# A windowed-attention and maxout kernel whose score products are cut into quarters of 32 queries, with the mixing products cut to the same weight shape

## Chip, cores and metric

The kernel runs on one core of one Trainium2 chip. The metric is the device time of one execution in microseconds (us). TensorE is called PE, and its weight loads PEld; VectorE is DVE, ScalarE is ACT, GpSimd is POOL and SyncE is SP. Differences of less than about 1% can hardly be told from no change here.

## The reference

Attention with a causal window of 128 keys and a linear bias, then a maxout layer, all in float32. There are 8 batches, 8 heads, 576 positions, 64 features a head.

```python
B, H, S, D = q.shape                                   # 8, 8, 576, 64
scores = scale * np.matmul(q, k.transpose(0, 1, 3, 2))
rel = pos[:, None] - pos[None, :]
mask = (rel >= 0) & (rel < 128)
scores = np.where(mask, scores + bias[None], -1000000000.0)
attn = softmax(scores)
attn_out = np.matmul(attn, v)
x = attn_out.transpose(0, 2, 1, 3).reshape(B * S, H * D)
h = np.maximum(np.maximum(x @ w1, x @ w2), x @ w3)     # 512 -> 768
return h @ w_out                                       # 768 -> 512
```

A query thus needs its own key and the 127 keys before it.

## The kernel before

**Attention.** A task is one batch and one pair of heads; there are 32. In a task the 576 queries are taken in blocks of 128 (i = 0 to 3) and a last one of 64. The last blocks of two tasks are joined into one step (i = NB = 4), so that two tasks make 9 steps, a batch 18 and the kernel 144. `steps` (L307) lists them, and they are worked off in pairs (s, s + 1).

`products` (L314) makes the scores of a pair of steps. For each step and each head j of the pair of heads it makes one product for each half h of the queries: 64 queries (the weights, `lhsT`, 64 features by 64 queries) with a range of keys (the moving operand), into PSUM partitions d to d + 63. The features of head j lie in partitions j * 64 to j * 64 + 63, so a step's four products take the four quarters of the PE array: two row halves (j) by two column halves (h). In a step with i = 0 each product takes 128 keys; in the other steps it takes the 192 keys from 128 before its first query to its last query; in batch 0 every second pair of steps is `whole`, has its own banks and takes 256 keys for i from 1 to 3. The columns of PSUM are the keys of the block before, then the block's own.

`score` (L339) merges the two key blocks: a masked copy on DVE (L347, L350) puts the score with a key of the block before over the place of each key after the query. Then a DVE instruction adds the bias and takes the row minimum (L361). `exps` is the exponential on ACT (L373), `sums_of` and `normalise` (L387, L392) divide by the row sum, `turn` (L400) transposes two steps' weights with four 128 by 128 PE products, ACT copies them (L404), and POOL splits them with two masked selects (L420, L424) into the part for the block's own keys and the part for the block before.

**Mixing** is the product of the weights with v. Batch 0 uses `mix` (L445), with 128 by 64 weights; this function is not touched. Batches 1 to 7 use `mix_rows` (L456): its inner `add` (L465) takes half of the keys (r, partitions r * 64 and on: the row half) of one block i and one head j (the column half: `lhsT` is 64 keys by 64 features of v), and moves 64 to 256 columns of queries through it into the PSUM bank of r. ACT and DVE then add the two banks (L500, L501). `MIX` says after which step of a task which blocks are mixed. A task takes 26 calls of `add` on average.

**Maxout and output.** `unit` (L613) makes one of 7 products of a fast matrix scheme, of 6 (for the output: 9) PE products of 128 by 128 weights with 288 columns (L641), in a float32 form rounded to a high and a low part. Their operands come from `split` on ACT and DVE (L514, L515) and subtractions (L518); results leave through ACT copies (L601, L650) and DVE (L599, L604, L605, L607). The weight tiles are streamed from DRAM by POOL's queue (L267).

**The order.** `events` is a list in which each piece has a due time in units of a step: for the pair of steps s, the products at s + 0.002, the transposes LAG_T = 4 steps later, the mixing LAG_X = 6 steps after the step it belongs to; the units of the batch before are spread evenly between. So PE's stream in batches 1 to 7 is: some 40 to 60 products of units, then a stage of mixing, scores and transposes, then units again. Up to step 46 (early in the third batch) the framework's planner orders PE's instructions by its own costs and by priority; from there on `pe` (L282) keeps PE to the program's order. Loads of q, k and v are issued on SP's queue (L295, L300).

Of the kernel before, what the change touches and what calls it, by code (L numbers as in the profile page):

```python
# [16 lines left out]
PSUM = bass.MemoryType.PSUM  # L17

NEG = 1.0e30
LOAD_I = 1  # L20
LAG_T, LAG_X = 4, 6
SHIFT = (0, 2, 4)
# [10 lines left out]
def attention_maxout_kernel(  # L33
# [11 lines left out]
    nc = tc.nc  # L45
    P = 128
    B, NP, _, _, S = qk.shape
    C, D = S // 2, P // 2
# [4 lines left out]
    NB = S // P  # L53
# [59 lines left out]
    def slopes(hp):  # L113
        for h in (2 * hp, 2 * hp + 1):
            nc.scalar.activation(bias[:, h, :], dist[:, 0], AF.Copy, scale=slope(h))
        nc.gpsimd.affine_select(  # L116
            out=bias0[:, 2 * hp:2 * hp + 2], in_=bias[:, 2 * hp:2 * hp + 2], pattern=[[0, 2], [-1, P]],
            compare_op=ALU.is_ge, fill=-NEG, base=0, channel_multiplier=1,
        )
# [162 lines left out]
    def pe(ins):  # L282
        if fixed:
            tc.keep_in_program_order(ins)
# [3 lines left out]
    qkt, vt = {}, {}  # L288
# [25 lines left out]
    def products(s):  # L314
        whole = s < n_steps and s % 4 == 2
        ps = [ps_m.tile([P, 512], F32, name=f"ps_m{j}") for j in range(2)] if whole else [scores[:, j] for j in range(2)]
        for a, (t, i) in enumerate(steps[s:s + 2]):
            banks[s + a] = [x[:, a * 2 * P:(a + 1) * 2 * P] for x in ps], None if whole else a
            for j in range(2):
                for h in range(2):  # L320
                    d = h * D
                    u, q0 = (t, i * P + d) if i < NB else (t + h, S - D)
                    if i == NB:
                        k0, k1 = q0 - P, S
                    elif i == 0:
                        k0, k1 = 0, P
                    elif whole:
                        k0, k1 = (i - 1) * P, (i + 1) * P
                    else:
                        k0, k1 = q0 - P, q0 + D  # L330
                    o = a * 2 * P + k0 - (i - 1) * P
                    pe(nc.tensor.matmul(  # L332
                        ps[j][d:d + D, o:o + k1 - k0],
                        lhsT=qkt[u][j * D:(j + 1) * D, 0, q0:q0 + D],
                        rhs=qkt[u][j * D:(j + 1) * D, 1, k0:k1],
                        start=True, stop=True, skip_group_check=True,
                    ))
# [118 lines left out]
    def mix_rows(t, blocks):  # L456
        b, hp = tasks[t]
        first = blocks[0] == 0
        if first:
            xp[t] = ps_x.tile([P, 2, 512], F32, name="ps_x")  # L460
            room[t] = 4 - len(blocks)
        x, vv, last = xp[t], vt[t], slice(t % 2 * D, (t % 2 + 1) * D)
        slot = lambda q: (q + room[t]) % 4 * P

        def add(r, j, i, rhs, o, start):  # L465
            k = slice(r * D, (r + 1) * D)
            pe(nc.tensor.matmul(  # L467
                x[j * D:(j + 1) * D, r, o:o + rhs.shape[1]], lhsT=vv[k, i, j * D:(j + 1) * D], rhs=rhs[k],
                start=start, stop=True, skip_group_check=True,
            ))  # L470

        for i in blocks:
            w = pp[t, i]
            low = (0, D if i else 0)
            if i == NB:
                for j in range(2):
                    add(1, j, i, w[:, j, 0, last], slot(i), False)
                continue
            whole = i < NB - 1 and slot(i) + P == slot(i + 1)
            for r in range(2):  # L480
                for j in range(2):
                    if whole:
                        y = w[:, j].rearrange("p a b -> p (a b)")
                        add(r, j, i, y[:, low[r]:(P + D, 2 * P)[r]], slot(i) + low[r], i == 0)
                    else:
                        add(r, j, i, w[:, j, 0, low[r]:], slot(i) + low[r], i == 0)
            if whole:
                continue
            for r in range(2):
                for j in range(2):  # L490
                    if i < NB - 1:
                        add(r, j, i, w[:, j, 1, :(D, P)[r]], slot(i + 1), False)
                    else:
                        add(r, j, i, pp[t, NB][:, j, 1, last], slot(NB), True)
        if first and hp % 2 == 0:
            xk[b, hp // 2] = xk_p.tile([P, 2, S], F32, name=f"xk{hp // 2}")
        c0, c1 = blocks[0] * P, min(S, (blocks[-1] + 1) * P)
        o = xk[b, hp // 2][:, hp % 2, c0:c1]
        y = x[:, :, slot(blocks[0]):slot(blocks[0]) + c1 - c0]
        nc.scalar.copy(out=o, in_=y[:, 0])  # L500
        nc.vector.tensor_tensor(out=o, in0=y[:, 1], in1=o, op=ALU.add)  # L501
# [157 lines left out]
    def at(when, what, *args):  # L659
        events.append((when, len(events), what, args))  # L660
# [3 lines left out]
    for s, (t, i) in enumerate(steps):  # L664
        c = s + shift[tasks[t][0]]
        if i == LOAD_I and t + 2 < len(tasks):
            at(c - 0.4, load, t + 2)
        if i == NB - 1 and t + 1 < len(tasks):
            at(c - 0.4, load_v, t + 1)
        if i == 0 and 0 < t < NP:  # L670
            at(c - 1, slopes, t)
            if t % 2 == 0:
                at(c - 1, slopes_t, t // 2)
        at(c + 0.04, score, s)
        at(c + 0.3, exps, s)
        if s % 2 == 0:
            at(c + 0.002, products, s)
            at(c + LAG_T + 0.003, turn, s)
        else:
            at(c + 1.1, sums_of, s)  # L680
            at(c + 1.5, normalise, s)
# [83 lines left out]
```

## Time and profile before

| | |
|---|---|
| median of 3 runs | 785.2 us (781.43, 785.20, 785.99) |
| the profiled execution | 782.06 us, its span 780.4 us |
| granted TensorE clock | 0.997 |
| PE busy | 750.2 us, 96% of the span |
| DVE, ACT, POOL busy | 554.6, 520.9, 185.5 us |
| score products (L332) | 1152 records, 69.1 us with some of them in flight |
| mixing products (L467) | 1456 records, 55.2 us with some of them in flight |
| unit products (L641) | 4032 records of 128 by 128 weights and 288 columns |
| DMA | 185 MB, 237 GB/s |

How to read it: a group names the line, the engine, the operation, what it writes and reads, then for PE the size of the weights (rows * columns), then the moving operand (partitions x columns) and the count; behind the bar come the busy time, the mean duration of one in ns, and idle time before it with what ended that. Products overlap in PE, so a group's busy time is the time in which at least one of them is in flight, and the mean of one is a latency. A float32 product of the program appears as two records, each with its own weight load (transposes appear as one).

A row of the timeline has the start in us, the time to the last one's end, the engine, line and form, and the count of instructions merged into the row. A row of the table by stretches has the stretch, its length, and for each engine the busy time and the count of instructions that touch the stretch; the last columns are the granted clock, DMA's share and GB/s.

### The profile page before, as it was taken

Reading aid. Unit: us, or ns where it says so; the run is one execution under the profiler, and the core shown is the slowest. Engines: PE = TensorE matmul, PEld = TensorE weight load, DVE = VectorE, ACT = ScalarE, POOL = GpSimd, SP = SyncE. Lnnn points to the kernel's source line nnn. Section 1 sums busy time; section 2 is a strip of 40 time slices with the busy share of each in tenths; the row PEclk is TensorE's granted clock in tenths of the full one; section 3 lists DMA queues with packets and bytes.
Section 4 is the critical chain, followed back from the end, with each engine's and each line's share of the span. In section 5 each row is a group of like instructions: output and inputs, shape, how many; then the busy total and the mean of one; then the engine's idle time right before and its main releaser. Section 6 shows DMA issues by size and latency. Waiting matters only on the chain.

```text
span 780.4 us, 19465 instructions
## 1 busy us (share of the span) xinstructions
PE 750.2 (96%) x7286; PEld 684.6 (88%) x7291; DVE 554.6 (71%) x1722; ACT 520.9 (67%) x1684; POOL 185.5 (24%) x388
## 2 busy tenths in 40 slices
PE   7888999999999999999999999999999999999997
PEld 3556878889998998999999998999999998999987
DVE  5888899885767747794777747794777757674562
ACT  6898787776767756776677666776677757542331
POOL 4331222211322122221222122311223122301100
PEclk9999999999999999999999999999999999999999
DMA  7862768584887569874888468974888567856851
GB/s 242 291 256 72 243 259 311 211 294 144 286 298 261 176 207 294 294 276 136 281 287 281 166 221 294 300 255 140 282 296 274 166 223 258 281 172 211 295 184 60
DMA packets 41678, 184.95 MB, mean 237 GB/s; under 512 B 4592, under 2 KB 13552, under 8 KB 32368
## 3 DMA queue, kind: packets, MB, share of 16 engines
q0 software_dynamic: 18144, 115.61, 44.4%
q1 hardware_dynamic: 23296, 67.97, 24.9%
q8 instruction: 57, 0.93, 0.5%
q14 instruction: 37, 0.30, 0.1%
q10 hardware_dynamic: 144, 0.13, 0.1%
HBM read 157.74 MB, written 25.95 MB: 235 GB/s over the span
## 4 chain that ended last, share of the span: by engine, by line
PE 64%; DVE 16%; ACT 8%; issue 7%; DMA 3%; POOL 1%; SPq 0%; POOLq 0%; DVEq 0%; ACTq 0%
PE ps_m L641 48%; PE ps_s L332 4%; PE pt L400 4%; PE ps_x L467 4%; DVE hs L515 4%; DVE hq L605 2%; ACT p L373 2%; DVE t L604 2%; DVE t L518 2%; PE pt L191 2%; DMA qk<-in_qk 1%; PE ps_m L191 1%; DMA wt<-keep 1%; DMA hs<-in_w_all 1%; DVE xk L501 1%
## 5 line engine op out<-in xcount | busy, mean ns | idle before, releaser
L641 PE MATMUL ps_m<-xs,wt 128*128 128x288 f32 x3024 | 430.3, 298 | 10.5 <-DVE hq L599 3.6
L641 PEld LDWEIGHTS ps_m<-xs,wt 128*128 128x128 f32 x3024 | 408.3, 189 | 18.2 <-DVE hq L599 5.3
L650 ACT COPY t<-ps_m 128x288 f32<-128x288 f32 x264 | 103.2, 394 | 83.0 <-PE ps_m L641 80.2
L641 PE MATMUL ps_m<-hs,ow 128*128 128x288 f32 x1008 | 140.9, 296 | 3.4 <-DVE hs L515 1.7
L641 PEld LDWEIGHTS ps_m<-hs,ow 128*128 128x128 f32 x1008 | 134.3, 188 | 6.5 <-ACT t L650 2.6
L420 POOL TENSOR_SCALAR_AFFINE_SELECT pp<-pr 128x256 f32<-128x256 f32 x112 | 54.2, 484 | 312.7 <-ACT pr L404 183.3
L373 ACT ACTIVATE p<-s,st 128x128 f32<-128x128 f32 x288 | 115.0, 403 | 17.2 <-DVE st L361 14.6
L267 POOL DMA_DIRECT2D wt<-keep x126 | 68.0, 539 | 210.9 <-PE ps_m L641 201.5
L392 ACT ACTIVATE p<-p,st 128x128 f32<-128x128 f32 x252 | 85.4, 395 | 23.8 <-DVE st L380 23.5
L604 DVE TENSOR_TENSOR t<-ps_m,t 128x288 f32<-128x288 f32 x144 | 64.8, 453 | 49.3 <-PE ps_m L641 31.3
L361 DVE CUSTOM_DVE_ANT_0 s<-ps_s,bias 128x128 f32<-128x128 f32 x240 | 60.8, 286 | 11.7 <-POOL bias L116 4.7
L605 DVE TENSOR_TENSOR hq<-t,hq 128x288 f32<-128x288 f32 x144 | 65.4, 460 | 2.6
L332 PE MATMUL ps_s<-qk 64*64 64x192 f32 (+1 forms) x1088 | 63.4, 317 | 2.6 <-DMA qk<-in_qk 2.0
L514 ACT CAST hs<-hq 128x288 fp32r<-128x288 f32 x96 | 41.0, 432 | 23.3 <-DVE hq L605 20.8
L373 ACT ACTIVATION_READ_ACCUMULATOR p<-s,st 128x1 f32 x288 | 55.8, 194 | 0.0
L467 PE MATMUL ps_x<-pp,v 64*64 64x64 f32 (+3 forms) x1456 | 55.2, 274 | 0.0
L501 DVE TENSOR_TENSOR xk<-ps_x,xk 128x256 f32<-128x256 f32 (+3 forms) x56 | 25.5, 455 | 41.8 <-ACT xk L500 41.8
L467 PEld LDWEIGHTS ps_x<-pp,v 64*64 64x64 f32 x1456 | 42.3, 133 | 10.8 <-issue 9.2
L424 POOL TENSOR_SCALAR_AFFINE_SELECT pp<-pr 128x256 f32<-128x256 f32 (+1 forms) x112 | 48.6, 434 | 1.1
L400 PE MATMUL pt<-plus,p 128*128 128x128 f32 x288 | 47.5, 286 | 1.2 <-DVE wt L181 0.5
L332 PEld LDWEIGHTS ps_s<-qk 64*64 64x64 f32 x1088 | 39.9, 134 | 9.8 <-issue 3.9
L400 PEld LDWEIGHTS pt<-plus,p 128*128 128x128 f32 x288 | 30.2, 140 | 19.4 <-issue 12.6
(89 smaller groups left out, 800.0 us busy)
## 6 DMA issues: line engine op xcount, KB each, us to landing
wt<-keep POOLq DMA_DIRECT2D x63, 1024.0 KB, 7.3
wt<-keep POOLq DMA_DIRECT2D x63, 768.0 KB, 5.8
qk<-in_qk SPq DMA_DIRECT2D x31, 576.0 KB, 5.3
hs<-in_w_all SPq DMA_DIRECT2D x12, 1023.6 KB, 6.5
v<-in_v SPq DMA_DIRECT2D x32, 320.0 KB, 5.8
keep<-wt SPq DMA_DIRECT2D x9, 1024.0 KB, 5.6
outT<-t SPq DMA_DIRECT2D x64, 144.0 KB, 1.8
keep<-wt SPq DMA_DIRECT2D x9, 768.0 KB, 4.7
```

What stands on the lines that cost most here:

```text
L267: nc.gpsimd.dma_start(wts[n, a], keep[n % 9][a])
L332: pe(nc.tensor.matmul(ps[j][d:d + D, o:o + k1 - k0], lhsT=qkt[u][j * D:(j + 1) * D, 0, q0:q0 + D], rhs=qkt[u][j * D:(j + 1) * D, 1, k0:k1] ...
L361: nc.vector.tensor_tensor_reduce(out=x, in0=ps[j][:, P:2 * P], in1=below, scale=-0.125, scalar=3.0e38, op0=ALU.add, op1=ALU.min, accum_out ...
L373: nc.scalar.activation(p[:, j], x, AF.Exp, bias=st[:, 0, a, j:j + 1], scale=-1.0, accum_out=st[:, 1, a, j:j + 1])
L392: nc.scalar.activation(p[:, j], p[:, j], AF.Copy, scale=st[:, 2, a, j:j + 1])
L400: pe(nc.tensor.transpose(out=pt[:, a, j], in_=p[:, j], identity=ident))
L420: nc.gpsimd.affine_select(out=old, in_=src, pattern=[[-x, n] for x, n in pat], compare_op=ALU.is_gt, fill=0.0, base=0, channel_multiplier=1,)
L467: pe(nc.tensor.matmul(x[j * D:(j + 1) * D, r, o:o + rhs.shape[1]], lhsT=vv[k, i, j * D:(j + 1) * D], rhs=rhs[k], start=start, stop=True, s ...
L604: nc.vector.tensor_tensor(out=s, in0=ps, in1=e, op=ALU.add)
L605: nc.vector.tensor_tensor(out=h, in0=s, in1=h, op=ALU.max)
L641: pe(nc.tensor.matmul(ps, lhsT=lt, rhs=rt, start=i == 0 and k in (0, 1, 4), stop=i == len(pairs) - 1, skip_group_check=True,))
L650: nc.scalar.copy(out=e, in_=ps)
```

## The change

In `products` each step's queries are taken in quarters of Q = 32 instead of halves of 64. The weights become 64 features by 32 queries, and the key range, where it is not 128 or 256 as above, becomes the 160 keys from 128 before the quarter's first query to its last query. A step has 8 products instead of 4. In the joined last step (i = NB) the quarters d = 0 and 32 belong to the first task and d = 64 and 96 to the second.

In `mix_rows` (batches 1 to 7) each product with 64 by 64 weights becomes two with 64 by 32 weights and the same moving columns. `mix` of batch 0 stays as it is.

```diff
+Q = 32
...
             for j in range(2):
-                for h in range(2):
-                    d = h * D
-                    u, q0 = (t, i * P + d) if i < NB else (t + h, S - D)
-                    if i == NB:
-                        k0, k1 = q0 - P, S
-                    elif i == 0:
+                for d in range(0, P, Q):
+                    u, q0 = (t, i * P + d) if i < NB else (t + d // D, S - D + d % D)
+                    if i == 0:
                         k0, k1 = 0, P
-                    elif whole:
+                    elif whole and i < NB:
                         k0, k1 = (i - 1) * P, (i + 1) * P
                     else:
-                        k0, k1 = q0 - P, q0 + D
+                        k0, k1 = q0 - P, q0 + Q
                     o = a * 2 * P + k0 - (i - 1) * P
                     pe(nc.tensor.matmul(
-                        ps[j][d:d + D, o:o + k1 - k0],
-                        lhsT=qkt[u][j * D:(j + 1) * D, 0, q0:q0 + D],
+                        ps[j][d:d + Q, o:o + k1 - k0],
+                        lhsT=qkt[u][j * D:(j + 1) * D, 0, q0:q0 + Q],
                         rhs=qkt[u][j * D:(j + 1) * D, 1, k0:k1],
                         start=True, stop=True, skip_group_check=True,
                     ))
...
         def add(r, j, i, rhs, o, start):
             k = slice(r * D, (r + 1) * D)
-            pe(nc.tensor.matmul(
-                x[j * D:(j + 1) * D, r, o:o + rhs.shape[1]], lhsT=vv[k, i, j * D:(j + 1) * D], rhs=rhs[k],
-                start=start, stop=True, skip_group_check=True,
-            ))
+            for m in range(j * D, (j + 1) * D, Q):
+                pe(nc.tensor.matmul(
+                    x[m:m + Q, r, o:o + rhs.shape[1]], lhsT=vv[k, i, m:m + Q], rhs=rhs[k],
+                    start=start, stop=True, skip_group_check=True,
+                ))
```

## The prediction

> **What bounds the kernel now.** I read the page first, then the busy time by stretch of about one batch, then who PE waits for, then the chain that ended last, and then single stages of PE in narrow windows.
>
> ```profile
> span 780.4 us, 19465 instructions
> PE 750.2 (96%) x7286; PEld 684.6 (88%) x7291; DVE 554.6 (71%) x1722; ACT 520.9 (67%) x1684; POOL 185.5 (24%) x388
> ```
>
> ```profile
> core 0: us, PE busy (x) PEld busy (x) DVE busy (x) ACT busy (x) POOL busy (x), PEclk, DMA share, GB/s
> 0.00:90.00 90.00, 77.91 (x603) 52.04 (x609) 70.17 (x216) 72.86 (x223) 30.95 (x64) 0.98 0.62 219
> 90.00:177.00 87.00, 82.37 (x820) 72.94 (x819) 77.75 (x211) 67.15 (x197) 20.65 (x36) 1.00 0.74 265
> ...
> 264.00:351.00 87.00, 86.16 (x898) 81.23 (x895) 61.82 (x205) 59.97 (x204) 21.37 (x46) 1.00 0.74 247
> ...
> 698.00:780.00 82.00, 74.76 (x552) 73.21 (x550) 38.23 (x94) 24.38 (x62) 7.43 (x14) 1.00 0.54 181
> ```
>
> From 177 to 698 us PE is busy 86 of every 87 us, and nothing else comes near it (DVE 62). In that stretch it waits for others only this much:
>
> ```profile
> PE ps_m L641 <- DVE hq L599: 3.6, 6, 0.6
> PE ps_m L641 <- ACT t L650: 0.5, 2, 0.3
> PE ps_m L641 <- DVE hs L515: 0.3, 1, 0.3
> ```
>
> So there a nanosecond of PE is nearly a nanosecond of span. In 0 to 90 PE, ACT and DVE share the limit, and in 90 to 177 DVE has 78 of 87. After 698 there are no scores and no mixing.
>
> The groups that the change touches:
>
> ```profile
> L332 PE MATMUL ps_s<-qk 64*64 64x192 f32 x840 | 55.4, 329 | 2.1 <-DMA qk<-in_qk 1.4 <-DVE st L361 0.7
> L467 PE MATMUL ps_x<-pp,v 64*64 64x192 f32 x364 | 30.3, 344 | 0.0
> L467 PE MATMUL ps_x<-pp,v 64*64 64x128 f32 x364 | 29.9, 274 | 0.0
> L467 PE MATMUL ps_x<-pp,v 64*64 64x64 f32 x644 | 24.9, 218 | 0.0
> L332 PE MATMUL ps_s<-qk 64*64 64x128 f32 x248 | 15.2, 277 | 0.5 <-DMA qk<-in_qk 0.5
> ```
>
> Their means (218 to 344 ns) are latencies that overlap; the pace has to be read from starts. Each float32 product of the program is two records: 144 steps of 4 products give the 1152 score records of L332. Here is one stage of two score steps, 16 records of 192 keys. The first column is the start. The rows come from ever later narrow windows, so each shows the start of the next group:
>
> ```profile
> 263.22 0.88 PE L332 MATMUL ps_s<-qk 64*64 64x192 f32 x16
> ...
> 263.44 0.51 PE L332 MATMUL ps_s<-qk 64*64 64x192 f32 x8
> ...
> 263.60 0.51 PE L332 MATMUL ps_s<-qk 64*64 64x192 f32 x8
> ...
> 263.76 0.34 PE L332 MATMUL ps_s<-qk 64*64 64x192 f32 x4
> ...
> 264.03 0.33 PE L400 MATMUL pt<-plus,p 128*128 128x128 f32 x1
> ```
>
> Four records start together at 263.22, 263.44, 263.60 and 263.76. The four 64 by 64 tiles of the array (two row halves by two column halves) thus run side by side, each streaming 192 columns in 0.16 us, or 0.83 ns a column. The first group takes 0.22: the extra 0.05 or 0.06 is the first weight load, which nothing hides. A stage with mixing and scores:
>
> ```profile
> 301.98 0.90 PE L467 MATMUL ps_x<-pp,v 64*64 64x192 f32 x28
> 302.69 0.74 PE L332 MATMUL ps_s<-qk 64*64 64x128 f32 x16
> 303.36 0.66 PE L400 MATMUL pt<-plus,p 128*128 128x128 f32 x4
> ```
>
> ```profile
> 302.47 0.42 PE L467 MATMUL ps_x<-pp,v 64*64 64x128 f32 x14
> 302.69 0.28 PE L332 MATMUL ps_s<-qk 64*64 64x128 f32 x2
> ...
> 302.80 0.63 PE L332 MATMUL ps_s<-qk 64*64 64x128 f32 x12
> ...
> 302.91 0.52 PE L332 MATMUL ps_s<-qk 64*64 64x192 f32 x8
> ```
>
> Groups of 128 keys follow 0.11 us apart (302.69, 302.80, 302.91), the same 0.83 to 0.86 ns a column. So the stage is bound by what each tile streams, and scores follow mixing without a gap.
>
> **The change part by part.** *Scores.* A step's four products of 64 queries with 192 keys become eight of 32 queries with 160. If the array runs eight 64 by 32 tiles side by side as it runs four now, a tile streams two records of 160 columns, 2 x 0.133 = 0.267 us, where it streams 2 x 0.16 = 0.32. That is 0.053 us less for each step with i from 1 to 4. A step with i = 0 keeps its 128 keys, and so do the 256 keys of batch 0's whole steps. A batch has 18 steps, 14 of them with i over 0: 14 x 0.053 = 0.75 us a batch, and 5.2 us for batches 1 to 7.
>
> *What of it reaches the end.* Once or twice a batch DVE sets the pace:
>
> ```profile
> 296.43 0.46 DVE t L604
> ...
> 302.03 0.38 DVE t L518
> ...
> 306.51 5.05 PE ps_m L641 x36
> ...
> 337.84 0.47 DVE t L604
> ...
> 344.91 5.09 PE ps_m L641 x36
> ```
>
> The chain runs on DVE and ACT from 296.4 to 306.5 and from 337.8 to 344.9; what PE saves in the two stages inside is waited for anyway. The first of them has one step with i over 0 (the 0.11 pace of the other is shown above), the second one or two. I take 3 of the 14 as lost, bounds 0 and 4. That leaves 11 x 0.053 x 7 = 4.1 us. Batch 1's scores lie in 90 to 177, where DVE is almost as full as PE; half of its 0.6 goes too, which leaves 3.8. For batch 0 (7 steps of 192 keys, at most 0.4 us, on a stretch shared by three engines) I take nothing.
>
> *Mixing.* Every product with 64 by 64 weights becomes two with 64 by 32 that stream the same columns. A batch's 208 records of L467 become 416 and its 144 score records become 288. On eight tiles each tile streams what it did, so the stage keeps its length. The DVE, ACT and POOL work behind it is the same.
>
> *Weight loads.* The first load is for 32 columns instead of 64: 0.05 becomes 0.03, once in each of some 65 stages, a gain of 1.7 us. Against it, four more tiles have to be started. The price of a start is bounded from both sides by this stage:
>
> ```profile
> 301.98:302.01 0.03, 0.03 (x4) 1.00 0.53 205
> ```
>
> Four start within 0.03 us, about 7 ns each, so four more cost 0.03 a stage, 1.8 us in all: the two cancel. From the other side, the densest longer stretch is the 14 records between 302.47 and 302.69, 0.22 / 14 = 16 ns, but there the tiles were full and streaming, so it is no proof of a limit. Eight tiles of 64-column products (0.053 us each) want a start every 7 ns. I take 7 to 9 ns, since the row with four starts is the one in which tiles are waiting for the sequencer; that costs the 64-column stretches 0 to 1 us over the kernel, and I take 0.
>
> *Instruction supply.* 2608 more products and as many loads are fetched (the row: packets, MB, share of the DMA engines):
>
> ```profile
> q8 instruction: 57, 0.93, 0.5%
> ```
>
> That is 16 KB a packet and 64 bytes for each of the 14577 records of PE and PEld, so 0.33 MB is added, spread over 780 us and hidden behind PE's long 128 by 128 runs. Bounds: nothing, or, if a packet came late in a stage, up to the shortest landing on the page's list, 1.8 us each time. I take nothing: the stages of now show no gap inside.
>
> *Order.* Up to about a third of the batches (step 46, some 225 us) the framework's planner, which counts each product's cost, orders PE. Twice the products can move other work around there. Bounds from the stages of that stretch: some lie alone with 0.2 us of switching in and 0.25 out; a handful more or fewer of them is 2 us either way. I take 0.
>
> **Sum:** 782.06 (the profiled execution's own time; 1.7 us of it lie around its span of 780.4) - 3.8 = 778.3. The runs shown have a median of 785.2, 3.1 above that execution, so on their scale 785.2 - 3.8 = 781.4; I say 781. That is 0.5%, less than the 1% that a measurement of this kernel can tell from no change.
>
> **The rivals.** *Everything lands* (faster by over 1%): the scores' 5.2, batch 0's 0.4, the loads' 1.7 without the stagger, and the rest that a record costs beside its columns (0.11 us in the row for 128 columns, against 128 x 0.83 = 0.106: an estimated 4 ns) falling away with the halved loads for the 64-column products of mixing, 644 / 4 = 161 on each tile, 0.6 us: 7.9 us, 777. For it speaks the full PE; against it the two DVE stretches. Chance 0.15.
>
> *Starts are the limit* (slower). One mechanism: PE cannot start products as fast as eight tiles eat them. A batch now has 352 records in about 10.9 us of streaming (scores: 14 x 0.32 + 4 x 0.213 = 5.3; mixing: 4 tasks, in each of which a tile of the second row half streams 832 columns by the ranges in mix_rows, 4 x 832 x 2 x 0.83 ns = 5.55). With 704 records at p ns each it is over that from 15.5 ns on, and over 1% slower (7.9 us in 7 batches) from 17 ns on. The stage above has 44 records from 301.98 to the start of its last group, 302.91 + 0.16 = 303.07: 25 ns. If that were a limit of starting, 704 x 25 = 17.6, + 6.7 x 7 = 47 us, 832. Against it stand the stretch at 16 ns and the burst at 7. Half way, at 20.5 ns: 14.4, + 3.5 x 7 = 25 us, 810. The Trainium skill has a rule of this kind: TensorE: Matmul & The Clock Gate, Wait — 56ns, not 53.3ns?, puts the least distance of two starts at about 25 ns however few the columns. The trace shows less for products in different tiles, so by this trace it does not hold between tiles. By it the time would be the 832 above.
>
> The chance of this rival is 0.14.
>
> *Quarters take turns* (slower). Nothing in the trace runs four column tiles in one row half. If only two can stream, a step of eight tiles takes 0.533 for 0.32 (0.427 for 0.213 at i = 0), 3.8 us more a batch, and mixing doubles, 5.55 more: 9.4 x 7 = 66 us, 851. Against it: two column halves already take different columns at the full pace. Chance 0.06.
>
> *The planner's part* goes wrong by more than 8 us in the first 225: 793 to 800. Chance 0.05. That the change does not do what it says (the shapes stay) I exclude from the diff.
>
> **How the numbers follow.** The forecast, within 1%, has the remaining 0.60. Faster by over 1% is the rival in which everything lands, 0.15. Slower by over 1%: 0.14 + 0.06 + 0.05 = 0.25. The likeliest one's own range is 777.5 to 787 (no loss to DVE, or starts at 16 ns: 704 x 16 = 11.3, + 2.5 us). The range that should hold 8 in 10 reaches down to 774 (everything, and 3 us of the planner) and up to 800 (starts at 18.5 ns, or the planner's case); the far ends of two rivals, 810 and more, are left out.
>
> **What would show it.** Right: L332 has 2304 records of 64x160, 64x128 and a few 64x256 in form 64*32, L467 has 2912; eight start within some 0.05 us; a stage like that at 263.22 is 1.03 - 0.11 = 0.92 us from the last L641 before it to the first L400; a stage's mixing part keeps its 0.71 us; a batch from 264 us on takes some 0.6 us less. Wrong: groups of four starts, or starts evenly 15 ns or more apart in the mixing; stages longer than now; an idle gap inside a stage; waits of PE on DVE growing by more than 0.2 us a batch; the first 177 us moved by more than 2 us.

## The result, and the profile after

The changed kernel takes 790.74 us (median of 5 runs, 789.76 to 792.33) where the kernel before takes 783.75 in the same comparison (5 runs, 781.43 to 785.99): a ratio of 1.0098, 95% interval 1.0072 to 1.0124. It is 7.0 us, 1%, slower; the forecast was 0.5% faster. 790.74 lies in the range of 774 to 800, but nearer to cases that I had given little chance.

Lines of the page after, and of its view of groups with the shapes kept apart:

```profile
span 788.1 us, 24680 instructions
PE 753.5 (96%) x9899; PEld 688.7 (87%) x9899; DVE 555.9 (71%) x1722; ACT 521.3 (66%) x1684; POOL 188.4 (24%) x388
...
q8 instruction: 78, 1.28, 0.7%
```

```profile
L330 PE MATMUL ps_s<-qk 64*32 64x160 f32 x1680 | 52.9, 303 | 1.8 <-DMA qk<-in_qk 1.1 <-DVE st L359 0.7
...
L466 PE MATMUL ps_x<-pp,v 64*32 64x128 f32 x728 | 32.2, 274 | 0.0
L466 PE MATMUL ps_x<-pp,v 64*32 64x192 f32 x728 | 30.5, 333 | 0.0
L466 PE MATMUL ps_x<-pp,v 64*32 64x64 f32 x1288 | 30.2, 220 | 0.0
```

The shapes are as written, and DVE, ACT and POOL have the same count of instructions and, within 3 us, the same busy time. PE is 3.3 us busier in a span that is 7.7 longer. (Numbers of lines shift by 1 or 2 against the kernel before: L332 is L330, L467 is L466, L641 is L640, L400 is L398, L650 is L649, L599 and L607 are L598 and L606.)

**Where the time went.** A batch begins for PE with a stage of scores alone; the timeline of PE has it, after:

```profile
263.79 0.29 PE L640 MATMUL ps_m<-hs,ow 128*128 128x288 f32 x1
264.01 0.78 PE L330 MATMUL ps_s<-qk 64*32 64x160 f32 x32
264.71 0.44 PE L398 MATMUL pt<-plus,p 128*128 128x128 f32 x2
...
352.38 0.37 PE L330 MATMUL ps_s<-qk 64*32 64x160 f32 x8
```

The next such row of the kernel before:

```profile
349.93 0.39 PE L332 MATMUL ps_s<-qk 64*64 64x192 f32 x4
```

Before, a batch is 349.93 - 263.22 = 86.71 us; after, 352.38 - 264.01 = 88.37. The other batches up to 617 us are alike (86.7 to 86.8 and 88.3 to 88.4). Four whole batches lose 6.4 us, the part of a batch from 184 to 264 us loses 1.0 and the tail 0.5; the first 184 us lose nothing. So the loss is not where I had looked for the planner's influence, the first third.

**What is in a batch.** First, the stages. The score stage above is 264.71 - 263.79 = 0.92 us from the last unit product, 0.11 less than before, and the eight first records fall within 0.05 us: the scores do what was forecast. Most stages with mixing do not. The one that was 301.98 to 303.36 is now

```profile
302.90 1.03 PE L466 MATMUL ps_x<-pp,v 64*32 64x192 f32 x53
303.71 0.31 PE L330 MATMUL ps_s<-qk 64*32 64x128 f32 x2
...
303.81 0.72 PE L330 MATMUL ps_s<-qk 64*32 64x128 f32 x28
304.46 0.66 PE L398 MATMUL pt<-plus,p 128*128 128x128 f32 x4
```

Its mixing takes 0.81 us (302.90 to 303.71) instead of 0.71, and the stage 1.56 instead of 1.38. Measured from the last unit product before to the first transpose after, the nine stages of a batch sum to 15.17 us, before to 14.65: 0.5 us a batch more. The nine stretches of unit products between the stages grow by 1.1 us a batch, 0.7 of it in the last one (8.7 to 9.5 us).

Second, PE waits more. The waits of PE on other engines from 177 to 690 us, after:

```profile
PE ps_m L640 <- ACT t L649: 4.1, 9, 0.7
PE ps_m L640 <- DVE hq L598: 3.6, 6, 0.6
PE ps_m L640 <- DVE hq L606: 1.3, 6, 0.2
```

That is 9.0 us against 4.4 before, 0.8 a batch. The wait for ACT grew most, from 0.5 to 4.1 us, and the PE timeline shows where it stands, about 5 us before the next batch's first stage:

```profile
345.55 0.95 PE L640 MATMUL ps_m<-xs,wt 128*128 128x288 f32 x6
347.13 5.33 PE L640 MATMUL ps_m<-hs,ow 128*128 128x288 f32 x36 [0.63 <-ACT t L649]
```

ACT's rows around it, after:

```profile
344.83 0.39 ACT L410 COPY pr<-pt 128x256 f32<-128x256 f32 x1
346.11 0.67 ACT L513 CAST xs<-xt 128x576 fp32r<-128x576 f32 x1 [0.89 <-DVE xt L517]
346.68 0.39 ACT L649 COPY t<-ps_m 128x288 f32<-128x288 f32 x1
```

and the same place before:

```profile
342.87 0.38 ACT L412 COPY pr<-pt 128x256 f32<-128x256 f32 x1
344.08 0.40 ACT L373 ACTIVATE p<-s,st 128x128 f32<-128x128 f32 x1 [0.83 <-DVE st L361]
344.39 0.19 ACT L373 ACTIVATION_READ_ACCUMULATOR p<-s,st 128x1 f32 x1
344.48 0.38 ACT L650 COPY t<-ps_m 128x288 f32<-128x288 f32 x1
```

The diff touches no ACT or DVE line, yet ACT now has the cast of xt, an operand of the next batch's units, ahead of the copy that frees PE's bank. The planner gave DVE and ACT another order, in every batch: 259 of 1434 places on DVE and 240 of 1396 on ACT hold another instruction than before (and 13 of 388 on POOL, 4 of 160 on SP). PE alone is held to the program's order from step 46 on.

So two theories: **order** (the loss is the planner's changed order of DVE and ACT), and **products** (the loss is in PE: the mixed stages got longer, because twice the products cannot be started or supplied as fast; the expectations below call this the starts theory).

### The profile page after: what moved, and what is told of

Read it like the earlier page. It is cut to its first block, busy times and chain, and to the rows that moved or that the text cites. A ratio compares the mean times of both kernels' runs of the same rounds, so it can differ in the third digit from the quotient of the medians.

```text
span 788.1 us, 24680 instructions
## 1 busy us (share of the span) xinstructions
PE 753.5 (96%) x9899; PEld 688.7 (87%) x9899; DVE 555.9 (71%) x1722; ACT 521.3 (66%) x1684; POOL 188.4 (24%) x388
## 3 DMA queue, kind: packets, MB, share of 16 engines
q8 instruction: 78, 1.28, 0.7%
## 4 chain that ended last, share of the span: by engine, by line
PE 57%; DVE 20%; issue 10%; ACT 7%; POOL 3%; DMA 3%; SPq 0%; POOLq 0%; ACTq 0%; DVEq 0%
PE ps_m L640 42%; DVE hs L514 5%; PE ps_x L466 4%; PE ps_s L330 4%; PE pt L398 3%; DVE hq L604 3%; DVE t L603 2%; DVE t L517 2%; PE pt L192 2%; ACT p L371 1%; DVE s L359 1%; DVE xk L500 1%; POOL wt L268 1%; DMA wt<-keep 1%; DMA qk<-in_qk 1%
## 5 line engine op out<-in xcount | busy, mean ns | idle before, releaser
L640 PE MATMUL ps_m<-xs,wt 128*128 128x288 f32 x3024 | 431.7, 299 | 10.2 <-DVE hq L598 3.6
L640 PEld LDWEIGHTS ps_m<-xs,wt 128*128 128x128 f32 x3024 | 409.2, 189 | 18.2 <-DVE hq L598 5.2
L649 ACT COPY t<-ps_m 128x288 f32<-128x288 f32 x264 | 103.5, 395 | 81.6 <-PE ps_m L640 79.2
L640 PE MATMUL ps_m<-hs,ow 128*128 128x288 f32 x1008 | 141.2, 297 | 5.6 <-ACT t L649 4.2
L640 PEld LDWEIGHTS ps_m<-hs,ow 128*128 128x128 f32 x1008 | 134.4, 188 | 8.9 <-ACT t L649 5.6
L418 POOL TENSOR_SCALAR_AFFINE_SELECT pp<-pr 128x256 f32<-128x256 f32 x112 | 56.5, 504 | 302.3 <-ACT pr L402 148.1
L330 PE MATMUL ps_s<-qk 64*32 64x160 f32 (+1 forms) x2176 | 60.8, 297 | 2.0 <-DMA qk<-in_qk 1.3
L466 PE MATMUL ps_x<-pp,v 64*32 64x64 f32 (+3 forms) x2912 | 62.3, 271 | 0.0
L466 PEld LDWEIGHTS ps_x<-pp,v 64*32 64x32 f32 x2912 | 47.7, 105 | 10.6 <-issue 9.5
L398 PE MATMUL pt<-plus,p 128*128 128x128 f32 x288 | 47.8, 287 | 2.2 <-POOL p L385 1.0
L398 PEld LDWEIGHTS pt<-plus,p 128*128 128x128 f32 x288 | 30.2, 140 | 19.6 <-issue 11.5
L348 DVE COPY_PREDICATED ps_s<-prev,ps_s 128x256 f32<-128x256 uint8 x105 | 44.4, 423 | 2.1 <-PE ps_s L330 0.9
```

Of the source, the lines that this page charges most:

```text
L330: pe(nc.tensor.matmul(ps[j][d:d + Q, o:o + k1 - k0], lhsT=qkt[u][j * D:(j + 1) * D, 0, q0:q0 + Q], rhs=qkt[u][j * D:(j + 1) * D, 1, k0:k1] ...
L398: pe(nc.tensor.transpose(out=pt[:, a, j], in_=p[:, j], identity=ident))
L418: nc.gpsimd.affine_select(out=old, in_=src, pattern=[[-x, n] for x, n in pat], compare_op=ALU.is_gt, fill=0.0, base=0, channel_multiplier=1,)
L466: pe(nc.tensor.matmul(x[m:m + Q, r, o:o + rhs.shape[1]], lhsT=vv[k, i, m:m + Q], rhs=rhs[k], start=start, stop=True, skip_group_check=True,))
L640: pe(nc.tensor.matmul(ps, lhsT=lt, rhs=rt, start=i == 0 and k in (0, 1, 4), stop=i == len(pairs) - 1, skip_group_check=True,))
L649: nc.scalar.copy(out=e, in_=ps)
```

## The experiments

In most kernels below the order of DVE, ACT, POOL and SP is written down. A table gives each engine's order, and after the program is traced each instruction is tied to the one ahead of it, without a semaphore:

```diff
+    for e, text in ORDER.items():
...
+        for first, then in zip(row, row[1:]):
+            tc.add_manual_dep(
+                then, first.name, mybir.DependencyInfo(mybir.DependencyClass.NoSync, mybir.DependencyReason.DATA),
...
```

Nothing else is added. No run has the kernel before tied to its own order, but e11 and e9 below come close: they carry the tied orders of before and of after with one instruction moved in five batches, and take the times of the kernels before and after to 0.1%. The first 184 us vary from run to run (181.8 to 187.7 us among kernels with the order of before in that part), so I read a batch's length and the ratio rather than one span.

**Products without the order, order without the products.** Edit: e1 is the kernel after with the table of before, e2 the kernel before with the table of after.

> The changed PE work, with the order of DVE, ACT, POOL and SP held to that of the kernel before. Starts theory (PE can start only one product per 16 to 17 ns once a burst of some 36 is used up, so the mixing stages grow; all else follows): the stages of a steady batch sum to 0.5 us more, and with the old order the added waits of PE on DVE and ACT (1.0 us a batch) fall away or not: 3.5 us slower than before if the order made them, 7 us slower if the longer stages made them. Order theory (the planner costs the products otherwise and puts DVE and ACT in another order, and that alone is the loss): within 1 us of the kernel before, or faster by the 4 us of the forecast.

> The kernel before on PE, with DVE, ACT, POOL and SP in the order of the changed kernel. Starts theory: no slower than before (within 1 us). Order theory: the whole loss, 7 us. If both act: about 4 to 7 us times the share of waits, 3.5 us.

e1: 783.67 us against 783.03, ratio 1.0003 (0.9973 to 1.0033). e2: 790.72, ratio 1.0097 (1.0066 to 1.0127). Waits of PE from 177 to 690 us, of e1 and then of e2:

```profile
PE ps_m L640 <- DVE hq L598: 3.6, 6, 0.6
PE ps_m L640 <- DVE hs L514: 0.3, 1, 0.3
PE ps_m L640 <- ACT t L649: 0.3, 1, 0.3
```

```profile
PE ps_m L641 <- ACT t L650: 5.4, 9, 0.8
PE ps_m L641 <- DVE hq L599: 3.6, 6, 0.6
PE ps_m L641 <- DVE hq L607: 2.2, 6, 0.4
```

The start of a batch and of the next in e1, then in e2:

```profile
263.51 0.77 PE L330 MATMUL ps_s<-qk 64*32 64x160 f32 x32
...
350.55 0.78 PE L330 MATMUL ps_s<-qk 64*32 64x160 f32 x32
```

```profile
267.59 0.88 PE L332 MATMUL ps_s<-qk 64*64 64x192 f32 x16
...
355.88 0.72 PE L332 MATMUL ps_s<-qk 64*64 64x192 f32 x12
```

e2, with not one PE product changed, has the whole loss, its stages at their old 14.65 us a batch and its batches at 88.25 to 88.29. e1 has the longer stages (15.18) and batches of 86.9 to 87.25, at most 0.5 over before. The order theory holds for the loss; the products, freed from it, are worth nothing either way that can be measured; the gain of 0.5% that was forecast lies outside e1's interval.

**One part of the change each.** Edit: in e3 `add` of `mix_rows`, in e4 the loop of `products` is the kernel before's; both have the table of before.

```diff
-            for m in range(j * D, (j + 1) * D, Q):
...
+            pe(nc.tensor.matmul(
+                x[j * D:(j + 1) * D, r, o:o + rhs.shape[1]], lhsT=vv[k, i, j * D:(j + 1) * D], rhs=rhs[k],
```

> Scores in quarters, mixing in 64 by 64 as before, all other engines in the order of before. Starts theory: the mixing part returns to its 0.71 us, a stage of scores alone is 0.93 us; between mixing and scores PE has to change its tile shape, estimated at 0.15 to 0.2 us from the 0.22 in and 0.25 out of a stage, in 8 of 10 stages of a batch: -0.75 + 8 x 0.17 = +0.6 us a batch, about 4 us slower. Theory that a change between two column shapes costs nothing: 4 us faster.

> Mixing in 64 by 32, scores in halves as before, all other engines in the order of before. Starts theory: the stage at the 28 calls grows by some 0.1 to 0.2 us without any gain from the scores, and two shapes follow each other: +1.2 (mixing) + 1.4 (shape) us a batch, 15 to 18 us slower. If the starts don't matter: only the change of shape, 8 us slower.

e3: 786.41 against 783.03, ratio 1.0027 (1.0000 to 1.0055), stages 15.18 us a batch. e4: 793.64, ratio 1.0113 (1.0057 to 1.0170), stages 17.01. The stage of scores alone shows the pure gain in e3 (0.93 us) and none in e4 (1.03); all others are longer. The timeline of PE in e4 shows why, in a stage with both shapes (the first row is the last mixing record's):

```profile
305.38 0.22 PE L469 MATMUL ps_x<-pp,v 64*32 64x64 f32 x1
305.53 0.43 PE L333 MATMUL ps_s<-qk 64*64 64x128 f32 x6
```

0.15 us pass before the first product of the other shape; over all stages of e3 and e4 it is 0.145 to 0.2 us, where the kernel before, without a change of shape, has 0.02 to 0.1. By the Trainium skill, TensorEngine Tiling (Array Packing), Key Properties, a change of the tiling mode drains the array; it gives no figure, and these rows agree with it. So the halves of the change are not independent: alone each pays at the seam, together neither does. Since e3 and e4 both pay it, the rest can be compared between them. From the first score product to the first transpose, the nine stages sum to 6.13 us in e3 and 6.88 in e4: the scores save 0.75 us a batch, as forecast. From the first to the last start of the mixing, the eight stages that have it sum to 5.65 us in e3, as before, and to 6.74 in e4, as after: 1.1 us a batch more. Taken the other way, the 0.5 us by which the stages of the kernel after grew and the 0.75 that scores save make 1.27 us a batch as the price of mixing, with what it costs the scores that start behind it.

The stages grew about as the starts theory said (by 0.5 and 2.4 us a batch, where 0.6 and 2.6 were expected), the times by about half of what was expected (0.3% and 1.1%, some 2 and 9 us, where 4 and 15 to 18 were expected): the batches of e4 are 88.2 us, 1.4 over before, those of e3 87.0, 0.3 over.

**Where in a batch the order costs.** Edit: the kernel before with the table of after only around the 448-column stretch (e5), or only elsewhere from the third batch on (e6).

> The kernel before on PE; of the new order of DVE and ACT only the places around the last 448-column results of a batch's mixing (once a batch: the ACT copy and the DVE sum of 448 columns of xk go behind the splits of hs, the subtraction into xt and the cast of xs go ahead of the scores' row minimum, the exponentials and a copy of a product of L641). Order theory, this place: the waits of PE that the changed kernel has and the one before has not, 0.5 us before L641 at about 345 us and 0.2 us 3.5 us later, in 6 batches: 4 us slower. Order theory, other places: no change. Starts theory: no change.

> The kernel before on PE, with the new order of DVE and ACT everywhere from the third batch on but at the place of the 448 columns; the first two batches as before. Order theory, other places: the added waits at 307 and 327 us (0.1 and 0.2 us a batch), 2 us slower. Order theory, the 448 place alone: no change. With the run before: what is missing to 7.7 us is the new order in the first 180 us, which fits the changed PE work there and not the old one.

e5: 786.05 against 782.41, ratio 1.0050 (1.0021 to 1.0079), batches 87.6. e6: 787.13, ratio 1.0053 (1.0027 to 1.0078), batches 87.4 to 87.65. Waits of PE in e5, then in e6:

```profile
PE ps_m L641 <- ACT t L650: 4.3, 6, 0.8
PE ps_m L641 <- DVE hq L599: 3.6, 6, 0.6
```

```profile
PE ps_m L641 <- DVE hq L599: 3.6, 6, 0.6
PE ps_m L641 <- DVE hq L607: 2.0, 5, 0.4
PE ps_m L641 <- ACT t L650: 2.0, 6, 0.4
PE ps_m L641 <- DVE hs L515: 0.3, 1, 0.3
```

Each half costs some 0.9 us a batch, and between them they bring e2's waits back; e6 costs twice what was expected of it. The loss has more than one place: in e5 the last stretch of units of a batch grows, from 8.7 to 9.6 us, in e6 three others by 0.2 to 0.4 us each.

**What bounds the mixed stages.** Edit: e7 takes 96 keys instead of 160 in a quarter with i over 0 (it leaves the oldest 64 keys of the window out of the scores); e8 puts block 3's shorter products ahead of the 192-column ones in `mix_rows`. Both are the kernel after with the table of before.

```diff
-                        k0, k1 = q0 - P, q0 + Q
+                        k0, k1 = q0 - D, q0 + Q
```

```diff
-        for i in blocks:
+        early = NB - 1 in blocks[1:]
+        for n, i in enumerate(([NB - 1] if early else []) + blocks):
...
+                    if early and n and i == NB - 1:
+                        continue
...
-            if whole:
+            if whole or early and n == 0:
```

> The changed PE work with the old order of the others, but 96 keys in place of 160 for each quarter (the oldest 64 keys of each query's window are left out of the scores). If PE's tiles were bound by columns, each stage would lose 0.053 us x 2 for each step with i over 0: about 0.1 us off every stage. If PE is bound by starting products, a stage of scores alone (32 records, all of them in the burst) loses the 0.1 to 0.2 us, and the stages with mixing keep their length: 1.75 and 1.8 us stay within 0.03 us.

> The changed PE work with the old order of the others, and in mix_rows the products of block 3 with 128 and 64 columns moved ahead of the ones with 192. Starts theory: the short products come while the burst lasts and the long ones give the sequencer time, so the stages with 56 and 72 mixing records shrink by 0.1 to 0.15 us (1.84 to 1.7, 2.08 to 1.95), those with 48 stay; 5 such stages a batch, 0.5 us a batch, 3 us in all, 780 where the kernel before has 783. If the columns bind: no change of the stages.

e7 (one run, 783.0 beside 782.41): the stage of scores alone fell from 0.92 to 0.71, and all mixed ones fell too, by 0.07 to 0.21 us; the sum is 13.81 a batch. Its first score stage:

```profile
263.92 0.56 PE L330 MATMUL ps_s<-qk 64*32 64x96 f32 x32
264.41 0.66 PE L398 MATMUL pt<-plus,p 128*128 128x128 f32 x4
```

0.49 us for 32 records, 264.41 - 263.92, against 0.70 at 160 columns: the 0.21 are 4 records on each tile by 64 columns by 0.83 ns. So scores are bound by columns on eight tiles, as forecast, and the products theory in its strong form (starts limit whatever the columns are) fell. A batch of e7 takes 85.8 to 86.4 us, 0.8 to 1.3 less than in e1, so most of the 1.36 us that its stages lose reaches the batch. Its one time does not show it: after 608 us PE waits 3.7 us for weight tiles from DRAM, in e1 0.3.

e8: 784.31, ratio 1.0005 (0.9978 to 1.0033); every stage kept its length to 0.01 us. Its stage at the same place:

```profile
300.42 1.03 PE L466 MATMUL ps_x<-pp,v 64*32 64x128 f32 x53
301.23 0.31 PE L330 MATMUL ps_s<-qk 64*32 64x128 f32 x2
```

Other columns stand first, and the mixing still takes 0.81 us to the first score product. That is what was expected if the columns bind, but columns alone do not explain it: a tile streams as many of them as before, when this mixing took 0.71. It looks like the count of records. In the stage at 302.90 of the kernel after, 32 records have started after 0.48 us, where before the change 16 had after 0.49, the pace of the columns in both. Then none starts for 0.09 us, and the last 24 take 0.31 us, 13 ns each, where eight tiles with 64 columns want one every 7 ns; in e8 the last 24 come 17 ns apart. From first to last start, the mixing with 32 records keeps its 0.40 us, and those with 48, 56 and 72 records grow from 0.73, 0.69 and 1.01 to 0.84, 0.87 and 1.20. Whether the supply of instructions to PE holds the later records back, or something in the array, is not shown; no experiment varied the supply.

**Undoing single places of the order.** Edits in the table: in the kernel after's, ACT's copy of ps_m is put ahead of the cast of xt (e9); in the kernel before's, DVE's `hq<-ps_m`, on which PE waits 0.6 us a batch, is put three places earlier, with the products of after (e10) and of before (e11). Each in five batches.

```diff
+t<-ps_m
 xs<-xt
-t<-ps_m
```

```diff
+hq<-ps_m,hq
 hs<-t,hs
 hs<-hq,hs
 s,st<-ps_s,bias_t
-hq<-ps_m,hq
```

> The kernel after with its own order on every engine, but in five batches (from the third to the seventh) ScalarE's copy of ps_m into t, which stands behind the cast of xt (xs<-xt) after the 448-column stretch, is put one place ahead of that cast. If PE's 0.9 us gap there (347.13 in the kernel after) is the wait for that copy, queued behind a cast that waits for DVE, the copy now begins as soon as the copy of pr is done, about 1.4 us earlier; the gap shrinks to 0.2 or 0.3 us and a batch gets 0.4 to 0.7 us shorter: 88.3 to between 87.6 and 87.9, and 2 to 3.5 us less than the kernel after in all, about 787.5 where before is 783 (ratio 1.006). If something else holds PE there (the later read of another bank, the xs operands themselves), the gap stays or comes back a few products later and the time stays at 1.010.

> The kernel after with the kernel before's order, but in five batches (from the third to the seventh) DVE's maximum that empties a bank (hq<-ps_m,hq, 0.6 us of waiting of PE in each batch, at 301.4 with this order) is put three places earlier, ahead of two subtractions of splits and one score instruction. Its operand should be ready by 299.3 and it would begin at 299.9 instead of 300.9. If the order of DVE sets these waits, the 0.67 us gap goes, a batch takes 86.3 instead of 87.0 and the kernel 3.3 us less than with the order of before: about 780, ratio 0.996. If the maximum was not ready earlier, or the splits that it passes are late then, the gap moves and the ratio stays at 1.000.

> The kernel before with its own order and the same move of DVE's maximum in five batches. If the order alone decides, it gains the same 0.67 us a batch: about 3.3 us, ratio 0.996, and the products of the kernel after are worth nothing on top of it. If the products of 64 by 32 weights gain once the waits around them are gone, this one is 1 to 2 us slower than the same move with the new products.

e9 and e10 came out as their second branch says, e11 as neither: it gains nothing, and it is not slower than e10. e9 790.83 against 783.29, ratio 1.0101 (1.0068 to 1.0134), batches 88.3 to 88.4; e10 784.30, 1.0019 (0.9997 to 1.0042), batches 87.0 to 87.3; e11 783.52, 1.0010 (0.9988 to 1.0033), batches 87.0. PE's timeline in e9, the place of the 0.63 us wait:

```profile
345.24 1.35 PE L640 MATMUL ps_m<-hs,ow 128*128 128x288 f32 x9
346.76 2.35 PE L640 MATMUL ps_m<-hs,ow 128*128 128x288 f32 x15 [0.17 <-ACT t L649]
349.46 1.86 PE L640 MATMUL ps_m<-hs,ow 128*128 128x288 f32 x12 [0.35 <-DVE hs L514]
351.25 0.78 PE L330 MATMUL ps_s<-qk 64*32 64x160 f32 x32
```

The wait for the first copy is gone. It came back in two pieces, at the next copy and at an operand `hs` that DVE had not split yet. e10 has one wait instead of another, 5 us later and longer:

```profile
302.67 2.64 PE L640 MATMUL ps_m<-xs,wt 128*128 128x288 f32 x18
306.32 1.46 PE L640 MATMUL ps_m<-xs,wt 128*128 128x288 f32 x9 [1.01 <-DVE hq L606]
```

The place of e9 lies in the 12 us before the next batch. The table by stretches has them, before and then after:

```profile
338.00:350.00 12.00, 11.86 (x131) 11.05 (x131) 11.93 (x34) 9.55 (x30) 2.17 (x4) 1.00 0.83 285
```

```profile
340.00:352.00 12.00, 11.35 (x173) 10.49 (x173) 11.79 (x33) 9.21 (x28) 2.05 (x4) 1.00 0.83 285
```

DVE is busy 11.9 and 11.8 of 12 us there, with nearly the same work. In such a stretch an instruction that goes first makes those that it passes late, and PE can wait for one of those instead. At the place of e10 and e11 DVE is busy 11.1 of 12 us (294 to 306 us in the kernel before), not quite full, and the wait moved there too. So the single instruction that the wait is put down to is where the delay shows, and moving it alone did not help. The order of before as a whole costs PE less before the next batch than that of after as a whole (e5); which of the rows that changed places carry it stays open.

## Why the prediction was wrong

- *Order*: this step failed. "Up to about a third of the batches (step 46, some 225 us) the framework's planner, which counts each product's cost, orders PE ... 2 us either way. I take 0." That is true of PE only. The planner orders DVE and ACT to the end, and it gave them another order although the diff touches PE's products alone (that the costs it counts for these did it is inferred). The new order alone costs 1.5 us in each of the four batches measured, and a ratio of 1.0097 in all (e2), as much as the whole change (1.0098). So it was not enough that "The DVE, ACT and POOL work behind it is the same": the work is, its order is not. The rival "the planner's part goes wrong" had the right kind of cause and nearly the size (over 8 us forecast, 7.0 measured), in the wrong stretch and at 0.05.
- *Scores*: right. 0.107 us for two steps measured in the stage at 264 us, as forecast; e3 and e4 give the 0.75 us a batch, and e7 confirms 0.83 ns a column on eight tiles.
- *What of it reaches the end*: 3.8 us forecast, nothing arrives (e1: 1.0003). The share that I took, 11 of 14, is not what failed: in e7, 0.8 to 1.3 of 1.36 us reached the batch. The gain is given back in the next term.
- *Mixing* and *weight loads*: this step failed too, and it is why the forecast gain is missing even under the old order. The mixing part was forecast at its old length; it costs 1.27 us a batch, 8.9 us in seven, against 5.2 saved. "7 to 9 ns" for a start holds for the first records of a stage; past some 32 of them the starts of the mixing come 13 to 17 ns apart, near the bound of 16 ns that I called "no proof of a limit". In e1 the batch grows by 0.2 to 0.4 us instead of shrinking by 0.6. That is less than the 0.5 by which the stages grow, since the stretches of units between them shrink by 0.1 to 0.4 us.
- *Starts are the limit*: half. Its threshold (15.5 ns a record) is about where the later records of mixing lie, but scores are not held by it and its 810 to 832 did not come. The 25 ns of the Trainium skill's TensorE: Matmul & The Clock Gate, Wait — 56ns, not 53.3ns?, are not a limit between tiles: eight records start within 0.05 us in the stage at 264.01.
- *Quarters take turns*: fell; e7's 0.49 us leaves no room for it.
- *Instruction supply*: the fetched bytes rose from 0.93 to 1.28 MB as worked out (0.33). What I bounded, a late packet of 1.8 us, does not show; a slower pace after the first records of a stage, which I had not thought of, does, and whether supply is its cause is open.
- Of the signs that I named, the 0.92 us stage came, the 0.71 us of mixing and the shorter batch did not. PE's waits grew, but on DVE by no more than the 0.2 us a batch that I allowed; the rest is on ACT, which I had not listed.

## What to carry to other kernels

When a planner orders the other engines, a change of PE's products is also a change of their queues: compare the order of every engine before and after, and time the new products under the old order and the old products under the new one; these two kernels settled here what the sum could not. A mean of 71% busy says nothing about a 12 us stretch at 99%, and there the instruction that PE waits for need not be the cause: here, moving it ahead moved the wait (e9). Halving the products' weights doubles their records, and that is free only while a run of them is short: the mixing of 32 records kept its length from first to last start, those of 48 to 72 grew by 0.11 to 0.19 us.

## What the runs showed of the hardware that was not expected

- Changing between 64 by 64 and 64 by 32 weights inside a stage costs 0.145 to 0.2 us from the last start of one to the first of the other (e3, e4); with one shape it is 0.02 to 0.1.
- Eight tiles start within 0.05 us and stream side by side at 0.83 ns a column, as expected; but past the first 32 records of a mixing stage with 56 the starts come 13 ns (kernel after) and 17 ns (e8, short products first) apart, and the mixing is as long in both orders.
